# Operands of the output projection split early and stored ready-made, and the sums of w_down spread over two stages of a fused attention and GLU kernel

## The chip, the core and the metric

One core of one Trainium2 chip runs the whole kernel. The metric is the device time of one launch in microseconds (us). All arithmetic is fp32; matmuls take operands split into two fp32r parts, a high part and a rest, and form three products of these parts.

## The reference

```python
def _A_ref(x, wqkv, w_phi, wo):
    qkv = transpose((x @ wqkv).reshape(B, S, 3, H, Dh))
    q, k, v = qkv[0], qkv[1], qkv[2]
    pq = einsum("bhsd,hdf->bhsf", q, w_phi)
    pk = einsum("bhsd,hdf->bhsf", k, w_phi)
    phi_q = concat([softmax(pq), softmax(-pq)])
    phi_k = concat([softmax(pk), softmax(-pk)])
    kv = einsum("bhsf,bhsd->bhfd", phi_k, v)
    z  = einsum("bhsf->bhf", phi_k)
    num = einsum("bhqf,bhfd->bhqd", phi_q, kv)
    den = einsum("bhqf,bhf->bhq", phi_q, z)[..., None] + 1e-6
    return (num / den) reshaped to (B, S, D) @ wo
def _B_ref(x, w_gate, w_up, w_down):
    h = sigmoid(x @ w_gate) * (x @ w_up)
    return h @ w_down
xn = layernorm(x)
return x + _A_ref(xn, ...) * silu(_B_ref(xn, ...))
```

S is 2048, D is 1024, 32 heads of 32, F is 3584.

## The kernel before

Every large product is done by a seven-product scheme on 2 x 2 blocks (named B11, T2, T3, B21, T1, T4, B22). Three of the seven weight operands are raw blocks (B11, B21, T4 for the projections and wo) and four are sums of blocks (T2, T3, T1, B22). The sums are made on POOL (GpSimd), four `tensor_tensor` instructions of 128x512 for each set, and stored in HBM. An operand that comes from HBM unsplit is split just before use: `split` (L123 and L124) is a cast on ACT to the high part and a subtraction on DVE for the rest. TensorE (PE) then runs `mm3` (L128 to L130): three matmuls of 128x512 for each pair.

The work has these stages, in order of time. The sequence is two chunks of 1024 rows.

- Projections of chunk 0 (V, K, Q; 21 steps of 48 matmuls, numbered n = 0 to 20), beside which x is normalised and transposed and the weights of K and Q are folded (`fold`).
- The gated linear unit (GLU) of chunk 0: 28 units of 7 steps of 12 matmuls. Background tasks from the queue `bg` run beside it.
- Projections of chunk 1, with eight background tasks on keys (`k_task`) beside them.
- The GLU of chunk 1. Beside it run the other key tasks, and tasks from a second queue `bg2`: four `o_sums` (the sums of wo) and fourteen `wd_sums` (the sums of w_down), one at every tenth step (`m % 10 == 0`). Each loads four blocks of 256 KB, makes four sums on POOL and stores them.
- The down projection (h times w_down), 56 double steps and 14 single ones, with the attention's denominators (`q_task`) beside it.
- The attention numerators and the output projection with wo, eight pairs of row tiles.

In the down projection's last part, `wo_prep` (L607) loads each of the 28 operands of wo, raw or summed, 256 KB, into one of the two halves of slot 53 and splits it into its place. A load into a half waits until the split before it has read that half.

SBUF is a set of numbered slots of 128 x 1024 fp32, used by name of block: fa is slots 39 to 42, fb 43 to 46, fc 47 to 54, w 28 to 35 (a ring of eight slots for split weights; a projection step uses four, a GLU step one). All DMAs are issued from SP's queue, in one order. ACT, DVE, POOL and SP each take their instructions in a fixed order that a scheduler writes at build time, so an instruction that waits holds all behind it on its engine.

The names `fc<-wf_d` and `fc<-wo` in the profile are the loads of `wo_prep`; `fb<-wo` and `fb<-w_down` are those of `o_sums` and `wd_sums`; L229 to L232 and L522 to L525 are their POOL sums; `p L124` is the subtraction of the key tasks, whose results the matmuls of L448 read. L841 and L848 to L851 are POOL's work on the GLU's own results, L885 on those of the down projection.

Of the kernel before, what the change touches and what calls it, by code (L numbers as in the profile page):

```python
# [9 lines left out]
F32 = mybir.dt.float32  # L10
F32R = mybir.dt.float32r
# [6 lines left out]
P = 128  # L18
# [7 lines left out]
NJ = NF // 2  # L26
HB = 512
EPS_LN = 1e-5
EPS_DEN = 1e-6
Q, K, V, O = 0, 1, 2, 3  # L30
# [14 lines left out]
B11, T2, T3, B21, T1, T4, B22 = range(7)  # L45
# [3 lines left out]
def hedgehog_glu_kernel(  # L49
# [11 lines left out]
    nc = tc.nc  # L61
# [4 lines left out]
    dram = ctx.enter_context(tc.tile_pool(name="dram", bufs=1, space=DRAM))  # L66
# [1 line left out]
    ident = sb.tile([P, P], F32, name="ident")  # L68
    make_identity(nc, ident)

    wf_d = dram.tile([4, 7, P, 4, HB], F32, name="wf_d")
    qkv_d = dram.tile([3, TT, 2, P, HB], F32, name="qkv_d")
    xo_d = dram.tile([7, P, 4, HB], F32, name="xo_d")
    e_d = dram.tile([TT, 2, P, 2 * HB], F32, name="e_d")
# [9 lines left out]
    slots, blocks, where = {}, {}, {}  # L84
# [22 lines left out]
    def whole(i):  # L107
        return slots[i].rearrange("p a n -> p (a n)")

    def halves(*ids):  # L110
        return [slots[i][:, a] for i in ids for a in range(2)]

    def run(i, n):

        name, k = where[i]
        return blocks[name][0][:, k:k + n]

    def pair(i):
        return slots[i][:, 0], slots[i][:, 1]

    def split(o, src):

        nc.scalar.copy(o[0], src)  # L123
        return nc.vector.tensor_sub(o[1], src, o[0].bitcast(F32))  # L124
# [94 lines left out]
    fraw = Ring(halves(43, 11))  # L219
    fblock = {K: Ring(((4, 5), (6, 7))), Q: Ring(((50, 51), (52, 53)))}  # L220

    def w_sums(which, k, a11, a12, a21, a22):
        def keep(i, b):
            nc.sync.dma_start(wf_d[which, i, :, k], b)

        if which != O:
            for i, b in ((B11, a11), (B21, a12), (T4, a22)):
                keep(i, b)
        nc.gpsimd.tensor_add(a22, a21, a22)  # L229
        nc.gpsimd.tensor_sub(a21, a11, a21)  # L230
        nc.gpsimd.tensor_sub(a11, a22, a11)
        nc.gpsimd.tensor_sub(a12, a12, a11)  # L232
        for i, b in ((T2, a11), (T3, a21), (T1, a22), (B22, a12)):
            keep(i, b)
# [22 lines left out]
            nc.sync.dma_start(wf_d[V, i], row4(v_first[i]))  # L257

    def o_sums(k, bs):
        for b, (f, h) in zip(bs, ((0, 0), (0, 1), (1, 0), (1, 1))):  # L260
            nc.sync.dma_start(b, wo[(k + 4 * h) * P:(k + 4 * h + 1) * P, f * HB:(f + 1) * HB])
        w_sums(O, k, *bs)

    def fold(which, k):

        bs = halves(*fblock[which].next())
        for b, (f, h) in zip(bs, ((0, 0), (0, 1), (1, 0), (1, 1))):
            r = fraw.next()
            nc.sync.dma_start(r, wqkT[which, f, k + 4 * h].rearrange("p g n -> p (g n)"))
            ps = tps.next()  # L270
            for g in range(4):
                gs = slice(g * P, (g + 1) * P)
                nc.tensor.matmul(ps[:, gs], r[:, gs], bd[:, 4 * f + g], start=True, stop=True)
            nc.scalar.copy(b, ps)
        w_sums(which, k, *bs)


    PROJ = (V, K, Q)
# [12 lines left out]
    flow = dict(item=0, made=0, used=0)  # L291
    proj_raw = Ring((39, 41))
    gr = Ring((41, 42, 39, 40))
    sums_r = Ring(halves(43, 44))
    wraw, proj_src, last_load = {}, {}, []
    units = [(c, j, s) for c in range(NCH) for j in range(NJ) for s in range(2)]
# [3 lines left out]
    def glu_load(u):  # L300

        c, j, s = units[u]
        a = []
        for f in (j, j + NJ):
            r = gr.next()
            k = 4 if c and f != j else 0
            nc.sync.dma_start(whole(r)[:, k * P:], w_gu[f, s, :, k:].rearrange("p k m -> p (k m)"))
            a += halves(r)
        wraw[u] = a

    def glu_sums(u):
        a11, a12, a21, a22 = wraw.pop(u)
# [50 lines left out]


    u1ps, u2ps = (halves(48, 49), halves(50, 51)), (halves(45, 46), halves(48, 49))
    yps = Ring(halves(47)), Ring(halves(43, 44, 45, 46))
    last_evac = []

    def proj_out(c, which, i, u, b):

        t = c * CTT + u
        u1p, u2p, yp = u1ps[c], u2ps[c], yps[c]

        def store(th, hb, y):
            nc.sync.dma_start(qkv_d[which, t + 4 * th, hb], y)

        def evac(y, x):
            last_evac[:] = [nc.vector.tensor_add(y, x, b).ins]

        if i == B11:  # L380
            nc.scalar.copy(u1p[u], b)
        elif i == B21:
            y = yp.next()
            nc.scalar.copy(y, b)  # L384
            store(0, 0, y)
        elif i == T2:
            evac(u1p[u], u1p[u])
        elif i == T3:
            evac(u2p[u], u1p[u])
        elif i == T4:  # L390
            y = yp.next()
            evac(y, u1p[u])
            store(0, 1, y)
        elif i == T1:
            evac(u2p[u], u2p[u])
            store(1, 1, u2p[u])
        else:
            y = yp.next() if c else u1p[u]
            evac(y, u1p[u])
            store(1, 0, y)  # L400
# [42 lines left out]
    def kv_products():  # L443

        while kv_due:
            t, ph, v = kv_due.popleft()
            for g in range(8):
                nc.tensor.matmul(kvb[g // 2][:, g % 2 * 256:g % 2 * 256 + 256], v[:, g].rearrange("p a f -> p (a f)"),  # L448
                                 ph[:, g].rearrange("p a f -> p (a f)"), start=t == 0 and g % 2 == 0,
                                 stop=t == TT - 1, skip_group_check=True)  # L450
# [66 lines left out]
    def wd_sums(j, b):  # L517
        b11, b12, b21, b22 = b
        for b, i in ((b11, B11), (b12, None), (b21, B21), (b22, B22)):
            nc.sync.dma_start(b, wd_block(i, j))  # L520
        sub = nc.gpsimd.tensor_sub
        sub(b11, b12, b11)  # L522
        sub(b12, b22, b12)
        sub(b22, b22, b11)
        sub(b21, b21, b22)  # L525
        for i, b in ((T1, b11), (T3, b12), (T2, b22), (T4, b21)):
            nc.sync.dma_start(wd_d[i, j], b)
# [38 lines left out]
    def q_task(t, hb):  # L566
# [5 lines left out]
        else:  # L572
# [22 lines left out]
    KVB = (36, 37, 38, 43)  # L595
    WO = {B11: list(range(8, 12)), T2: list(range(12, 16)), T3: list(range(4, 8)), B21: [],
          T1: [], T4: [], B22: list(range(4))}
    wor = Ring([slots[53][:, 0], slots[53][:, 1]])
    phu = Ring((44, 20))
    ofr = Ring((46, 24, 25, 26, 27, 22, 23, 39, 40, 41, 42))  # L600
    res = Ring(halves(49, 52))
# [3 lines left out]
    oraw = [slots[50], slots[51]]  # L605

    def wo_prep(i, k):  # L607
        r = wor.next()
        if i in (B11, B21, T4):
            f, h = {B11: (0, 0), B21: (0, 1), T4: (1, 1)}[i]  # L610
            nc.sync.dma_start(r, wo[(k + 4 * h) * P:(k + 4 * h + 1) * P, f * HB:(f + 1) * HB])
        else:
            nc.sync.dma_start(r, wf_d[O, i, :, k])
        split(pair(WO[i][k]), r)

    def e_load(u):
        tp_, hb = divmod(e_next[u], 2)
# [136 lines left out]
    bg, bg2 = deque(), deque()  # L754
# [3 lines left out]
    for hb in range(2):  # L758
        bg.extend([lambda hb=hb, t=t: k_task(hb, t) for t in range(TT)])
        bg.extend([lambda hb=hb, f=f: f(hb) for f in (kv_sum, kv_blocks, z_broadcast)])  # L760
    bg2.extend([lambda k=k: o_sums(k, halves(43, 44)) for k in range(4)])
    bg2.extend([lambda j=j: wd_sums(j, halves(43, 44)) for j in range(NJ)])
    EARLY = 8
    tick = [0, 0]
# [1 line left out]
    def background(anchor, tasks=None):  # L766
        if tasks is None:
            tasks = bg
            kv_products()
        if tasks:  # L770
            with tc.issue_after(anchor):
                tasks.popleft()()

    for n, (kind, c, what, i) in enumerate(ops):
        ws = ready[n]
        if kind == "proj":
            for u in range(4):
                if i in opening:
                    pbank[u] = pmm.next()
                xo = run(XO[i], 4)  # L780
                us = slice(u * P, (u + 1) * P)
                for k in range(4):
                    mm3(pbank[u], (xo[:, k, 0, us], xo[:, k, 1, us]), pair(ws[k]),
                        i in opening and k == 0, k == 3, skip_group_check=True)
                step()
            flow["used"] += 4
            while prep():
                pass
            for u in range(4):
                proj_out(c, what, i, u, pbank[u])  # L790
            if c and len(bg) > 2 * (TT + 3) - EARLY and i not in (B11, B21):
                background(last_evac[0])
            continue

        j, s = what
        u = units.index((c, j, s))
# [29 lines left out]
        else:  # L826
# [8 lines left out]
            else:  # L835
                if q == 0:
                    nc.vector.tensor_mul(g, g, bank)
                else:
                    b = u1 if q == 1 else u2
# [4 lines left out]
                else:  # L844

                    a11, a21, a12, a22 = gates
# [8 lines left out]
        m = (u % (2 * NJ)) * 7 + glu_order.index(i)  # L855
        if c == 0:
            if len(bg) > 2 * (TT + 3) and i == T2 and m > 7:
                background(v.ins)
        else:
            if m >= 1 and (m - 1) % 6 == 0:  # L860
                background(v.ins)
            if m >= 10 and m % 10 == 0:
                with tc.issue_after(last_load[0]):
                    background(v.ins, bg2)
        if c == 0 and u % (2 * NJ) == 2 * NJ - 1:
# [50 lines left out]
    for n, (i, j, cs) in enumerate(dsteps):  # L916
        w, hs = dready[n]
        for c in cs:
            for u in range(4):
                p = 4 * c + u  # L920
# [15 lines left out]
        if n and n * 32 // 78 > (n - 1) * 32 // 78 and late:  # L936
            t, hb = late.pop(0)
# [48 lines left out]
    for tp_ in range(NTP):  # L986
        nxt = attend(tp_ + 1) if tp_ + 1 < NTP else []
        n = 0
        u1, u2, y11, y21 = [res.next() for _ in range(4)]
        for i in range(7):  # L990
# [3 lines left out]
            o = [h.rearrange("p (k t) -> p k t", t=P) for h in pair(of[tp_][i])]  # L994
# [12 lines left out]
            else:  # L1007
                g, xt = gxs.pop((tp_, i))
                t, cols = rows(tp_, i)
                eng = nc.vector if tp_ == NTP - 1 and i in (T4, B22) else nc.gpsimd  # L1010
                if i == B21:
                    y = y11
                    nc.vector.tensor_mul(y, g, ps)
                else:
                    y = {T1: u2, T4: y21, B22: u1}[i]
# [34 lines left out]
```

## Time and profile before

| | |
|---|---|
| median of 3 runs | 2445.2 us (2442.9 to 2446.99) |
| the profiled execution | 2443.43 us |
| its span, first to last instruction | 2441.6 us |
| PE busy | 2392.8 us, 98% of the span |
| PE's granted clock over the span | 0.995 |

Busy time of PE is the union of its matmul records, so it is not time at PE's peak. In the tables by stretch of time, a line gives start and end in us, the length, and for each engine the busy time and, in brackets, the count of instructions; then PE's granted clock, the share of DMA time and GB/s. A line of a table of groups has busy us and the mean ns of one instruction, and behind the second bar the idle time before the group and what ended it.

### The profile page before, as it was taken

The page shows a single profiled execution, that of the slowest core. Times are in us where ns is not written, and L with a number is a line of the kernel's source. Part 1 is how long each engine was busy: PE and PEld are TensorE (multiplying, and loading weights), DVE is VectorE, ACT ScalarE, POOL GpSimd, SP SyncE. Part 2 cuts the span into 40 slices and gives each one's busy share as a digit, 9 for nine tenths or more (in the row PEclk, how much of TensorE's full clock was granted, in tenths as well). Part 3 has the DMA queues.
Part 4 walks back from the last instruction along what each step waited for, and adds up shares of the span by engine and source line. Part 5 has one row for each costly group of instructions (what it writes and reads, how often), then busy time and mean ns, then how long its engine had stood idle before and what let it go on. Part 6 is the DMA issues. An engine that isn't in the chain of part 4 may idle for free.

```text
span 2441.6 us, 31984 instructions
## 1 busy us (share of the span) xinstructions
PE 2392.8 (98%) x11076; PEld 1986.7 (81%) x11076; DVE 1716.9 (70%) x2247; ACT 1001.9 (41%) x1495; POOL 987.2 (40%) x665
## 2 busy tenths in 40 slices
PE   7999999999999999999999999999999999998998
PEld 6888888888888878888888888788888888877886
DVE  6533577777776678548858888647889998765554
ACT  6432244544444344323433444423443334454332
POOL 5520146566565400004545453543333335314554
PEclk8999999999999999999999999999999999999999
DMA  7874567777776665457888887896666766755553
GB/s 280 279 255 157 195 226 261 255 257 271 263 276 242 245 216 174 172 203 249 292 301 284 275 316 257 278 339 216 217 231 219 254 218 238 236 197 191 182 182 128
DMA packets 231507, 581.61 MB, mean 238 GB/s; under 512 B 30385, under 2 KB 30385, under 8 KB 226737
## 3 DMA queue, kind: packets, MB, share of 16 engines
q1 hardware_dynamic: 231344, 579.57, 68.7%
q8 instruction: 87, 1.43, 0.2%
q14 instruction: 76, 0.61, 0.1%
HBM read 353.76 MB, written 225.71 MB: 237 GB/s over the span
## 4 chain that ended last, share of the span: by engine, by line
PE 77%; DMA 7%; DVE 6%; issue 4%; POOL 4%; ACT 2%; SPq 0%; ACTq 0%; POOLq 0%; DVEq 0%
PE bank L128 25%; PE bank L130 25%; PE bank L129 25%; DVE x L124 1%; DMA fc<-wf_d 1%; DMA w<-ws_d 1%; PE bank L448 1%; DMA fa<-w_down 1%; PE bank L627 1%; DVE w L124 1%; DMA fb<-w_down 1%; DVE p L124 1%; DMA fb<-wo 1%; ACT x L123 1%; DMA fc<-xo_d 0%
## 5 line engine op out<-in xcount | busy, mean ns | idle before, releaser
L128 PE MATMUL bank<-x,w 128*128 128x512 f32 x2352 | 912.7, 390 | 5.1 <-DVE fb L833 3.1
L129 PE MATMUL bank<-x,w 128*128 128x512 f32 x2352 | 915.9, 389 | 0.5 <-DVE x L124 0.4
L130 PE MATMUL bank<-x,w 128*128 128x512 f32 x2352 | 906.7, 389 | 0.0
L123 ACT CAST w<-fa 128x512 fp32r<-128x512 f32 (+1 forms) x444 | 308.2, 698 | 560.3 <-PE bank L129 335.8
L124 DVE TENSOR_TENSOR w<-fa,w 128x512 fp32r<-128x512 f32 (+1 forms) x444 | 434.8, 984 | 140.7 <-ACT w L123 134.1
L128 PEld LDWEIGHTS bank<-x,w 128*128 128x128 f32 x2352 | 441.6, 188 | 98.6 <-DVE fb L833 4.4
L130 PEld LDWEIGHTS bank<-x,w 128*128 128x128 f32 x2352 | 441.6, 188 | 91.9 <-DVE w L124 0.4
L129 PEld LDWEIGHTS bank<-x,w 128*128 128x128 f32 x2352 | 441.7, 188 | 91.2 <-DVE x L124 1.2
L128 PE MATMUL bank<-w,x 128*128 128x512 f32 x708 | 279.2, 394 | 3.7 <-ACT fb L384 2.1
L130 PE MATMUL bank<-w,x 128*128 128x512 f32 x708 | 278.5, 394 | 1.8 <-DVE x L124 1.8
L129 PE MATMUL bank<-w,x 128*128 128x512 f32 x708 | 277.9, 393 | 0.0
L841 POOL TENSOR_TENSOR fc<-fc 128x512 f32<-128x512 f32 x27 | 43.6, 1615 | 298.9 <-DVE fc L840 286.8
L128 PEld LDWEIGHTS bank<-w,x 128*128 128x128 f32 x708 | 134.0, 189 | 31.8 <-ACT fb L384 2.5
L130 PEld LDWEIGHTS bank<-w,x 128*128 128x128 f32 x708 | 133.8, 189 | 30.0 <-DVE x L124 2.5
L129 PEld LDWEIGHTS bank<-w,x 128*128 128x128 f32 x708 | 134.0, 189 | 27.2 <-DVE w L124 0.2
L577 POOL TENSOR_TENSOR fc<-fc 128x1024 f32<-128x1024 f32 x32 | 81.4, 2543 | 178.3 <-ACT fc L413 123.1
L841 POOL TENSOR_TENSOR fb<-fb,fc 128x512 f32<-128x512 f32 x57 | 91.2, 1600 | 130.7 <-DVE fc L840 107.3
L317 POOL TENSOR_TENSOR fb<-fa 128x512 f32<-128x512 f32 x28 | 36.7, 1309 | 248.2 <-DMA fa<-w_gu 133.7
L124 DVE TENSOR_TENSOR w<-fb,w 128x512 fp32r<-128x512 f32 (+1 forms) x114 | 106.0, 929 | 39.2 <-ACT w L123 37.7
L123 ACT CAST w<-fb 128x512 fp32r<-128x512 f32 (+1 forms) x114 | 71.4, 627 | 133.6 <-PE bank L129 103.8
L124 DVE TENSOR_TENSOR x<-fa,x 128x512 fp32r<-128x512 f32 x112 | 111.1, 993 | 15.6 <-ACT x L123 15.3
L840 DVE TENSOR_TENSOR fc<-fc,bank 128x512 f32<-128x512 f32 x84 | 57.3, 683 | 89.8 <-PE bank L130 75.8
(250 smaller groups left out, 3312.2 us busy)
## 6 DMA issues: line engine op xcount, KB each, us to landing
ws_d<-w SPq DMA_DIRECT2D x112, 512.0 KB, 3.9
w<-ws_d SPq DMA_DIRECT2D x112, 512.0 KB, 5.4
fa<-w_gu SPq DMA_DIRECT2D x84, 512.0 KB, 4.2
fa<-h_d SPq DMA_DIRECT2D x84, 512.0 KB, 4.1
fa<-wf_d SPq DMA_DIRECT2D x32, 1024.0 KB, 5.3
h_d<-fc SPq DMA_DIRECT2D x120, 256.0 KB, 4.0
fc<-e_d SPq DMA_DIRECT2D x48, 512.0 KB, 3.9
fc<-qkv_d SPq DMA_DIRECT2D x80, 256.0 KB, 4.2
```

What stands on the lines that cost most here:

```text
L123: nc.scalar.copy(o[0], src)
L124: return nc.vector.tensor_sub(o[1], src, o[0].bitcast(F32))
L128: nc.tensor.matmul(o, a[0], b[0], start=first, stop=False, **kw)
L129: nc.tensor.matmul(o, a[0], b[1], start=False, stop=False, **kw)
L130: nc.tensor.matmul(o, a[1], b[0], start=False, stop=last, **kw)
L317: nc.gpsimd.tensor_add(s1, a21, a22)
L448: nc.tensor.matmul(kvb[g // 2][:, g % 2 * 256:g % 2 * 256 + 256], v[:, g].rearrange("p a f -> p (a f)"), ph[:, g].rearrange("p a f -> p (a ...
L577: nc.gpsimd.tensor_mul(ez, e, zb)
L627: nc.tensor.transpose(ps[:, j * P:(j + 1) * P], e[:, k * P:(k + 1) * P], ident)
L840: v = nc.vector.tensor_add(b, u2 if q == 3 else u1, bank)
L841: nc.gpsimd.tensor_mul(g, g, b)
```

## The change

- `o_sums` runs in the projections of chunk 0 (after steps n = 7, 10, 13 and 16) instead of the GLU of chunk 1, and in slots 52 and 53. It now splits all seven operands of a column block itself, one after the other through slot 54, and stores each split pair (512 KB) in a new array `wo_d`. `wo_prep` becomes one load of 512 KB straight into the operand's place; its 28 casts and 28 subtractions go.
- Nine of the fourteen `wd_sums` run in the projections of chunk 1 (after B21, T2 and T1 of V, K and Q); the other five in the GLU of chunk 1, at every fourteenth step.
- The ring for the projections' results in chunk 1 shrinks from eight to six halves. The GLU weights of chunk 1 get two rings: whole slots 39 and 40, and the four halves of 41 and 42.
- What runs from `bg2` is now queued on SP behind the last store of a projection result.

```diff
-    wf_d = dram.tile([4, 7, P, 4, HB], F32, name="wf_d")
+    wf_d = dram.tile([3, 7, P, 4, HB], F32, name="wf_d")
+    wo_d = dram.tile([7, 4, P, 2 * HB], F32, name="wo_d")
...
     def o_sums(k, bs):
         for b, (f, h) in zip(bs, ((0, 0), (0, 1), (1, 0), (1, 1))):
             nc.sync.dma_start(b, wo[(k + 4 * h) * P:(k + 4 * h + 1) * P, f * HB:(f + 1) * HB])
-        w_sums(O, k, *bs)
+        def keep(i, b):
+            o = slots[54].bitcast(F32R)
+            split((o[:, 0], o[:, 1]), b)
+            nc.sync.dma_start(wo_d[i, k], whole(54))
+        w_sums(keep, *bs)
...
+    gr1, gr1h = Ring((39, 40)), Ring(halves(41, 42))
...
+        if c:
+            r, h = gr1.next(), gr1h.next()
+            nc.sync.dma_start(whole(r), w_gu[j, s].rearrange("p k m -> p (k m)"))
+            nc.sync.dma_start(h, w_gu[j + NJ, s, :, 4:].rearrange("p k m -> p (k m)"))
+            wraw[u] = halves(r) + [None, h]
+            return
...
-    yps = Ring(halves(47)), Ring(halves(43, 44, 45, 46))
+    yps = Ring(halves(47)), Ring(halves(45, 46, 47))
...
-            nc.sync.dma_start(qkv_d[which, t + 4 * th, hb], y)
+            last_load[:] = [nc.sync.dma_start(qkv_d[which, t + 4 * th, hb], y).ins]
...
     def wo_prep(i, k):
-        r = wor.next()
-        if i in (B11, B21, T4):
-            f, h = {B11: (0, 0), B21: (0, 1), T4: (1, 1)}[i]
-            nc.sync.dma_start(r, wo[(k + 4 * h) * P:(k + 4 * h + 1) * P, f * HB:(f + 1) * HB])
-        else:
-            nc.sync.dma_start(r, wf_d[O, i, :, k])
-        split(pair(WO[i][k]), r)
+        nc.sync.dma_start(slots[WO[i][k]].bitcast(F32), wo_d[i, k])
...
-    bg2.extend([lambda k=k: o_sums(k, halves(43, 44)) for k in range(4)])
+    bg2.extend([lambda k=k: o_sums(k, halves(52, 53)) for k in range(4)])
     bg2.extend([lambda j=j: wd_sums(j, halves(43, 44)) for j in range(NJ)])
...
+            if (i in (B21, T2, T1)) if c else (n % 3 == 1 and n > 5 and len(bg2) > NJ):
+                with tc.issue_after(last_load[0]):
+                    background(last_evac[0], bg2)
...
-            if m >= 10 and m % 10 == 0:
+            if m >= 14 and m % 14 == 0:
                 with tc.issue_after(last_load[0]):
                     background(v.ins, bg2)
```

More of the change, by code (lines that the diff above doesn't have):

```diff
@@ L220, in hedgehog_glu_kernel, with w_sums @@
     fblock = {K: Ring(((4, 5), (6, 7))), Q: Ring(((50, 51), (52, 53)))}
[L222 to L228, printed above, removed]
+    def w_sums(keep, a11, a12, a21, a22):
+        for i, b in ((B11, a11), (B21, a12), (T4, a22)):
+            keep(i, b)
         nc.gpsimd.tensor_add(a22, a21, a22)
@@ L274, in fold @@
             nc.scalar.copy(b, ps)
-        w_sums(which, k, *bs)
+        w_sums(lambda i, b: nc.sync.dma_start(wf_d[which, i, :, k], b), *bs)
     PROJ = (V, K, Q)
@@ L302, in glu_load @@
         c, j, s = units[u]
-        a = []
+        if c:
[4 more added lines that the diff above has]
+            return
+        wraw[u] = []
         for f in (j, j + NJ):
             r = gr.next()
[L306 to L309, printed above, removed]
+            nc.sync.dma_start(whole(r), w_gu[f, s].rearrange("p k m -> p (k m)"))
+            wraw[u] += halves(r)
     def glu_sums(u):
@@ L597, in hedgehog_glu_kernel @@
           T1: [], T4: [], B22: list(range(4))}
-    wor = Ring([slots[53][:, 0], slots[53][:, 1]])
     phu = Ring((44, 20))
```

## The prediction

> **What bounds the kernel now.** I read the table by stretch of time first, cut at the stages, then PE's waits, then the chain of waits near the end.
>
> ```profile
> core 0: us, PE busy (x) PEld busy (x) DVE busy (x) ACT busy (x) POOL busy (x), PEclk, DMA share, GB/s
> 150.00:280.00 130.00, 130.00 (x575) 107.62 (x575) 50.41 (x57) 33.36 (x39) 0.00 (x0) 1.00 0.47 160
> 280.00:860.00 580.00, 580.00 (x2592) 480.89 (x2591) 417.45 (x556) 260.99 (x385) 334.57 (x226) 1.00 0.72 255
> ...
> 880.00:950.00 70.00, 70.00 (x325) 58.58 (x324) 65.80 (x82) 30.86 (x37) 0.00 (x0) 1.00 0.56 189
> 950.00:1097.00 147.00, 147.00 (x665) 122.33 (x664) 85.64 (x107) 45.57 (x53) 0.00 (x0) 1.00 0.52 179
> 1097.00:1330.00 233.00, 229.87 (x1053) 190.29 (x1053) 174.91 (x213) 94.22 (x130) 108.64 (x72) 1.00 0.81 280
> 1330.00:1600.00 270.00, 265.48 (x1217) 219.83 (x1217) 213.76 (x251) 114.82 (x154) 129.84 (x87) 1.00 0.84 287
> ...
> 2135.00:2196.00 61.00, 58.09 (x287) 46.97 (x286) 42.57 (x61) 35.13 (x64) 11.67 (x8) 1.00 0.59 198
> 2196.00:2257.00 61.00, 54.06 (x291) 44.18 (x290) 33.48 (x48) 24.69 (x45) 25.57 (x19) 1.00 0.59 190
> ...
> sum 2441.60, PE 2392.80 PEld 1986.66 DVE 1716.88 ACT 1001.87 POOL 987.23; mean PE 184.06 PEld 152.82 DVE 132.07 ACT 77.07 POOL 75.94
> ```
>
> TensorE is the bound: 2392.8 of 2441.6 us. The change adds and removes no matmul, so it can only win part of the 48.8 us in which PE stands idle, or add to them. The stages that it touches hold these parts: nothing in the later projections of chunk 0 (150 to 280) and in the projections of chunk 1 (880 to 1097), where PE is full; 3.1 and 4.5 us in the GLU of chunk 1 (233 - 229.87 and 270 - 265.48); 2.9 and 6.9 us around the end of the down projection (61 - 58.09 and 61 - 54.06). Together 17.4 us, which is the ceiling of any gain. The change takes work out of the two stages with idle PE and puts it into two stages where PE is full, and POOL there is at 0.00.
>
> **End of the down projection: what the 28 splits cost.** PE's waits from 2196 to 2257, ACT's waits in the same stretch, and a piece of the chain:
>
> ```profile
> PE bank L128 <- ACT fa L123: 1.7, 1, 1.7
> PE bank L128 <- DVE x L911: 1.6, 1, 1.6
> PE bank L128 <- DVE fc L1016: 1.1, 1, 1.1
> PE bank L128 <- ACT w L123: 1.0, 1, 1.0
> PE bank L128 <- ACT fb L123: 0.8, 1, 0.8
> PE bank L130 <- DVE fa L124: 0.6, 1, 0.6
> ...
> ACT x L123 <- DMA fc<-wf_d: 15.8, 4, 5.6
> ACT w L123 <- DMA fc<-wf_d: 4.1, 1, 4.1
> ```
> ```profile
> 2210.36 0.32 SPq L889
> ...
> 2210.78 4.62 DMA fc<-wf_d
> ...
> 2215.49 0.63 ACT x L123
> ...
> 2216.14 0.70 DVE x L124
> ...
> 2216.86 3.12 DMA fc<-wf_d
> ```
>
> ACT stands for 15.8 + 4.1 = 19.9 of 61 us at casts of `wo_prep` whose load has not landed. All behind them on ACT waits too: the casts of attention operands (fa, fb) for which PE waits. SP is held the same way: a load into a half of slot 53 goes only after the subtraction that reads it, and one turn of that loop took 2216.86 - 2210.78 = 6.08 us, 4.62 of it the landing and 1.46 the rest. The new `wo_prep` has no cast, no subtraction and no half to wait for. So of the six waits only the 1.6 on L911 (the last evacuation of the down projection) stays: 1.7 + 1.1 + 1.0 + 0.8 + 0.6 = 5.2 us go. Of the 2.9 idle us before 2196, where the same loop runs among the loads of w_down and h, I take half, 1.4. What is late next: the four direct loads of B22 go into slots 0 to 3 and wait for the last stores of the down projection, of which SP issues the last at 2210.36 (row above). A load of 512 KB takes about 5.4 us (row below).
>
> ```profile
> ws_d<-w SPq DMA_DIRECT2D x112, 512.0 KB, 3.9
> w<-ws_d SPq DMA_DIRECT2D x112, 512.0 KB, 5.4
> fb<-wo SPq DMA_DIRECT2D x16, 256.0 KB, 6.8
> ...
> 2200.52 0.50 PE L128 MATMUL bank<-x,fb 128*128 128x512 f32 x1 [1.60 <-DVE x L911]
> ```
>
> With 3.9 for the store's landing they leave at some 2210.4 + 3.9 = 2214.3 and land by 2220 to 2222. The output projection begins at 2200.5 and eight pairs fill the rest of the span, 241 / 8 = 30 us each; B22 is the last of seven products, so it is due near 2200.5 + 30 * 6/7 = 2226. That is 4 us to spare, so I take off a little: the stage gives **-6 us**, between -8 (all 2.9 go as well) and -1 (these loads, or those of T3 ahead of the h loads on SP, hold PE instead).
>
> **GLU of chunk 1.** PE's waits from 1097 to 1600, one of them looked at on POOL and DVE, and the same DVE instruction without POOL (950 to 1100) and beside it (1160 to 1560):
>
> ```profile
> PE bank L448 <- DVE p L124: 3.2, 4, 1.3
> PE bank L128 <- DVE fb L833: 3.1, 3, 2.4
> ...
> 1503.22 2.15 POOL L525 TENSOR_TENSOR fb<-fb 128x512 f32<-128x512 f32 x1
> ...
> 1504.15 2.31 DVE L124 TENSOR_TENSOR p<-fc,p 128x1024 fp32r<-128x1024 f32 x1
> ```
> ```profile
> L124 DVE TENSOR_TENSOR p<-fc,p 128x1024 fp32r<-128x1024 f32 x4 | 4.9, 1216 | 0.0
> L378 DVE TENSOR_TENSOR fc<-fc,bank 128x512 f32<-128x512 f32 x22 | 15.0, 684 | 15.8 <-PE bank L130 15.6
> ...
> L124 DVE TENSOR_TENSOR p<-fc,p 128x1024 fp32r<-128x1024 f32 x20 | 33.1, 1653 | 0.0
> L840 DVE TENSOR_TENSOR fc<-fc,bank 128x512 f32<-128x512 f32 x28 | 19.1, 683 | 26.2 <-PE bank L130 21.6 <-POOL fb L841 3.2 <-POOL fc L841 1.2
> ```
>
> PE waits for DVE, and DVE is late because POOL slows it: 1216 ns become 1653 on average and 2310 where a sum of w_down runs at that moment. An instruction with a PSUM operand keeps its 684 ns. The change takes four `o_sums` and nine `wd_sums` out of here, 52 POOL instructions, and their 104 DMAs. After step 70 no task of `bg2` is left, so of the 4.5 us after 1330 I take 2.7; before it five tasks run in place of seven, and I take 0.8 of 3.1. POOL's work on gates stays, and can delay DVE as before. **-3.5 us**, between -7 and 0. The new rings for the GLU weights only let the half loads go earlier; I cost them at nothing, hidden by the w ring.
>
> **Projections of chunk 0.** They get 16 loads, 16 sums, 28 casts, 28 subtractions and 28 stores. The engines have room: ACT is at 33 of 130 us, DVE at 50, POOL at 0, DMA at 0.47. The question is order. All 28 go through slot 54 in series, and a cast that waits for the store before it holds ACT, and with it the casts of the projection weights. One turn is the landing plus the 1.46 above: with 3.9 for a 512 KB store, 5.4 us. In the changed order on ACT, 22 pieces of projection weights (11 steps) stand between the first and the 21st of these casts. The cast of such a piece, before:
>
> ```profile
> L123 ACT CAST w<-fa 128x1024 fp32r<-128x1024 f32 x22 | 23.1, 1054 | 69.5 <-PE bank L130 69.4
> ```
>
> A step is 48 matmuls of 130 / 575 = 0.226 us, 10.85 us, so 11 steps take 119 us and 20 turns 107 us: the chain keeps up. Moreover a piece is ready some 2.4 us after its slot comes free (1054 ns of cast and near 1.2 us of subtraction; ACT waits for nothing but PE here) and due a step later, so some 8.4 us of delay cost nothing. The seven other turns stand between GLU pieces, of which eight are ready ahead. **+1 us**, between 0 and the rival below.
>
> **Projections of chunk 1.** Nine `wd_sums`: 36 loads, 36 sums on an idle POOL, 36 stores with DMA at 0.52 to 0.56. The sums slow DVE, which from 880 to 950 is busy for 65.8 of 70 us. Three tasks, 12 sums, fall there. At worst each costs one DVE instruction 2.31 - 1.22 = 1.09 us, together 13; I take half, 6.5. Against it stand DVE's 4.2 idle us and its lead:
>
> ```profile
> 947.20 1.22 DVE L124 TENSOR_TENSOR w<-fa,w 128x1024 fp32r<-128x1024 f32 x1
> ...
> 954.14 1.05 ACT L123 CAST w<-fa 128x1024 fp32r<-128x1024 f32 x1 [0.30 <-PE bank L130]
> ```
>
> The subtraction for the step that begins when PE returns slots at 954.1 ended at 948.4: 5.7 us of lead. So 6.5 us are covered by 9.9, and 13 are not, by 3. **+0.5 us**, between 0 and +3. After 950 DVE has 61 idle us of 147. SP queues the stores behind POOL's sums; the loads of projection weights behind them have a whole step of 10.85 us.
>
> **Sum.** -6 - 3.5 + 1 + 0.5 = -8. The profiled execution took 2443.4 us, so 2435.4; the median of the runs shown is 1.8 above that execution, and I forecast a median of 2437.2. About 0.2%, 5 us, is what a measurement of this kernel can tell from no change.
>
> **Rivals.** (1) *Slower: the chain through slot 54 sets the pace of chunk 0.* The landing decides: 20 turns fit into 119 + 8.4 us up to 4.9 us of landing. The 3.9 speaks against it, and it was taken mostly in the GLU of chunk 0, with the DMA share at 0.72; for it speak the 5.4 and 6.8 us of other transfers. At 5.4 the turns take 137 us, +10; at 6.8 they take 165 us, +38. With the gains of -9 elsewhere: 2446 to 2474, some 2456 in the middle. Chance 0.13.
>
> (2) *The waits only change hands.* The direct loads are twice as large and late by what the splits were, and DVE stays late by POOL's gate work: only some 3 us go, 2442. For it speaks that PE's waits in the GLU are short and many and that each has another instruction behind it. Chance 0.20.
>
> (3) *DVE in chunk 1 is held for whole sums.* If each of the 12 sums between 880 and 950 held DVE for its full 2.15 us (row above), that is 26 us, 16 past the cover of 9.9: 2445.2 - 9 + 16 = 2452. Against it speaks the mean of 1653, less than half of such a delay on one instruction. Chance 0.07. The Trainium skill, "SBUF — State Buffer", Who interferes with whom, states such a rule: a DVE instruction with two SBUF inputs and a GpSimd instruction that reads SBUF exclude each other for the whole instruction, whereas one with a single SBUF input does not contend. By that rule this case decides; the trace agrees on who is affected (1216 to 1653 ns with two SBUF operands, 684 and 683 with a PSUM operand), and on the size only at single instructions (2310).
>
> **Numbers.** The forecast has 0.60 and by itself 2430 to 2442: its ends are the full gains (-8 - 7) and gains of half size. Range 2430 to 2448, which takes in rival 2 and the lower part of rival 1. Faster 0.62 (the forecast and a little of rival 2), within 0.2% 0.22, slower 0.16 (most of rivals 1 and 3).
>
> **What would show it.** Right: no ACT wait for a load of wo after 2100 and PE idle near 3.5 us in the two stretches around the end of the down projection; in the GLU of chunk 1 the p subtraction nearer to 1216 ns and PE idle near 4 us; PE still full in both projection stages. Wrong: PE idle between 150 and 300 with ACT casts in fc that wait for a store to wo_d (rival 1); PE waits for the subtraction of w between 880 and 960 (rival 3); new PE waits on B22's load in the first pair (rival 2).

## The result, and the profile after

The changed kernel takes 2438.51 us (median of 20 runs, 2429.96 to 2443.7), the kernel before 2446.1 us (20 runs, 2442.9 to 2449.2): a ratio of 0.997, with a 95% interval of 0.9962 to 0.9978. That is 7.6 us less, and 1.3 us above the forecast. The profiled execution has a span of 2436.6 us at a granted clock of 0.996 (before 2441.6 us, 0.995).

The total came out as predicted, the parts did not: the loss in chunk 0 and the gains in the other stages were all far larger than forecast, and they offset each other. Here is the table by stretch of time of the changed kernel, in the stretches that were shown of before (line numbers are up to ten higher than before: the splits are L124 and L125, the three matmuls L129 to L131). Its stages begin up to 13 us later than before, so a stretch does not hold quite the same work.

```profile
core 0: us, PE busy (x) PEld busy (x) DVE busy (x) ACT busy (x) POOL busy (x), PEclk, DMA share, GB/s
150.00:280.00 130.00, 126.32 (x552) 103.04 (x551) 59.44 (x70) 40.91 (x56) 19.49 (x13) 1.00 0.72 242
280.00:860.00 580.00, 574.36 (x2560) 474.64 (x2560) 416.93 (x568) 259.69 (x385) 332.97 (x227) 1.00 0.75 264
...
880.00:950.00 70.00, 67.81 (x307) 55.31 (x306) 64.95 (x75) 28.09 (x32) 19.81 (x12) 1.00 0.81 278
950.00:1097.00 147.00, 146.97 (x668) 122.17 (x667) 100.17 (x111) 43.93 (x54) 38.48 (x24) 1.00 0.78 261
1097.00:1330.00 233.00, 231.55 (x1060) 192.21 (x1059) 176.08 (x217) 102.84 (x138) 85.95 (x58) 1.00 0.79 266
1330.00:1600.00 270.00, 270.00 (x1246) 225.08 (x1245) 206.45 (x257) 117.96 (x157) 77.55 (x52) 1.00 0.66 218
...
2135.00:2196.00 61.00, 59.21 (x296) 48.98 (x295) 36.43 (x53) 31.22 (x56) 9.05 (x7) 1.00 0.64 219
2196.00:2257.00 61.00, 61.00 (x336) 52.37 (x335) 30.80 (x42) 21.56 (x38) 28.53 (x21) 1.00 0.74 255
```

Idle PE (length less busy time) goes down from 3.1 and 4.5 to 1.5 and 0 us in the GLU of chunk 1, and from 2.9 and 6.9 to 1.8 and 0 around the end of the down projection. It goes up from 0 to 3.7 and 5.6 in chunk 0, and from 0 to 2.2 between 880 and 950.

Idle time understates a stall, though, and a second view shows it. These are the waits of PE's weight loads from 2196 to 2280 in the kernel before (first fence) and in the changed one (second): what is waited for, us in total, times, longest.

```profile
PEld bank L128 <- ACT fa L123: 2.5, 2, 2.2
PEld bank L128 <- DVE x L911: 1.8, 1, 1.8
PEld bank L128 <- ACT w L123: 1.4, 1, 1.4
PEld bank L128 <- DVE fc L1016: 1.3, 1, 1.3
PEld bank L128 <- ACT fb L123: 1.2, 1, 1.2
PEld bank L130 <- DVE fa L124: 1.1, 2, 0.9
...
```
```profile
PEld bank L630 <- DVE x L125: 0.9, 1, 0.9
PEld bank L131 <- DVE x L125: 0.7, 1, 0.7
```

The first is cut after its six largest rows, 9.3 us, against 1.6 us after. The same six rows are 6.8 us in the matmul rows that the prediction used. Why they differ is seen at any wait of PE, such as this one in the changed kernel:

```profile
290.05 0.39 PE L131 MATMUL bank<-w,x 128*128 128x512 f32 x1
291.07 0.50 PE L129 MATMUL bank<-w,x 128*128 128x512 f32 x1 [0.63 <-DVE fc L388]
```

The starts are 1.02 us apart where 0.226 us is the pace, so 0.79 us are lost; but the first record lasts until 290.44, and 0.63 us are shown as idle. Each wait loses some 0.16 us from view in this way, and waits shorter than that don't show at all.

So I measure the stages by landmarks instead: the first and the last copy of a B11 bank in the projections of chunk 1, and the first such copy in the down projection. The first pair is of the kernel before, the second of the changed one; the columns behind the count are the durations in ns (minimum, median, maximum) and the first and last start.

```profile
L381 ACT COPY fc<-bank x12: 568/578/589, 844.6 to 1012.5; 128x512 f32<-128x512 f32 x12
...
L896 ACT COPY x<-bank x8: 579/587/589, 1720.5 to 1726.0; 128x512 f32<-128x512 f32 x8
```
```profile
L391 ACT COPY fc<-bank x12: 568/582/589, 857.5 to 1026.3; 128x512 f32<-128x512 f32 x12
...
L902 ACT COPY x<-bank x8: 579/588/589, 1726.4 to 1731.8; 128x512 f32<-128x512 f32 x8
```

The four stages, in us, for this and, read in the same way, for all kernels of the experiments below:

| kernel | A: start to first B11 copy of chunk 1 | B: to the last (Q) | C: GLU of chunk 1, to the first B11 copy of the down projection | D: from there to the end | span |
|---|---|---|---|---|---|
| before | 844.6 | 167.9 | 708.0 | 721.1 | 2441.6 |
| changed | 857.5 (+12.9) | 168.8 (+0.9) | 700.1 (-7.9) | 710.2 (-10.9) | 2436.6 (-5.0) |
| two slots | 846.2 | 172.6 | 699.8 | 708.1 | 2426.7 |
| wo alone | 853.2 | 167.6 | 704.7 | 709.8 | 2435.3 |
| w_down alone | 845.4 | 170.0 | 703.0 | 723.8 | 2442.2 |
| before, no sums beside GLU | 845.2 | 167.4 | 697.9 | 721.3 | 2431.8 |
| two slots, no sums of w_down | 846.5 | 169.9 | 698.0 | 708.8 | 2423.2 |
| two slots, sums in K and Q | 845.4 | 165.7 | 702.6 | 708.5 | 2422.2 |
| changed, no sums of wo | 853.5 | 171.0 | 700.2 | 707.3 | 2432.0 |
| two slots again | 845.3 | 170.6 | 700.2 | 708.5 | 2424.6 |

Each is one execution. How far a stage differs between executions can be read where the code is the same: A is 844.6 to 846.5 without the single slot, and 853.2 to 857.5 with it; D is 721.1 to 723.8 with the splits at the end, and 707.3 to 710.2 without.

Two of the 12.9 us in A were lost before the first of the new casts ran (it starts at 159.08). This is the first B11 copy of K in chunk 0, before and in the changed kernel:

```profile
147.31 0.59 ACT L381 COPY fc<-bank 128x512 f32<-128x512 f32 x1 [1.66 <-PE bank L130]
```
```profile
149.31 0.59 ACT L391 COPY fc<-bank 128x512 f32<-128x512 f32 x1 [1.67 <-PE bank L131]
```

With two slots it starts at 149.05, so this part is not the slot's. From this copy to the end of A it is 696.5 to 697.3 us in the seven executions without the single slot, and 708.2 (changed), 705.7 (wo alone) and 705.3 (changed, no sums of wo) with it. The chain through the slot thus cost 10.9 us here, and 8.0 to 8.4 in the other two.

Where these 10.9 us went is seen in ScalarE's waits from 150 to 340 and in a piece of its timeline. The timeline's columns are start, duration, engine, line, instruction, and in brackets the idle time before it and what ended it.

```profile
ACT fc L124 <- DMA wo_d<-fc: 91.1, 23, 8.2
ACT fc L124 <- POOL fc L229: 9.4, 2, 4.8
ACT fc L394 <- DMA qkv_d<-fc: 6.3, 1, 6.3
...
311.80 0.62 ACT L124 CAST fc<-fc 128x512 fp32r<-128x512 f32 x1 [7.30 <-DMA wo_d<-fc]
...
315.19 0.62 ACT L124 CAST w<-fb 128x512 fp32r<-128x512 f32 x1 [1.21 <-POOL fb L328]
315.72 0.58 ACT L827 COPY fc<-bank 128x512 f32<-128x512 f32 x1
...
324.47 0.62 ACT L124 CAST fc<-fc 128x512 fp32r<-128x512 f32 x1 [5.96 <-DMA wo_d<-fc]
...
326.93 0.60 ACT L837 ACTIVATE fb<-bank 128x512 f32<-128x512 f32 x1
```
```profile
316.35 0.50 PE L129 MATMUL bank<-x,w 128*128 128x512 f32 x1 [1.81 <-ACT fc L827]
```

And PE's waits from 150 to 380 (before, there was none):

```profile
PE bank L129 <- DVE fc L388: 2.7, 4, 1.4
PE bank L129 <- ACT fb L837: 2.3, 1, 2.3
PE bank L129 <- ACT fc L394: 1.8, 2, 1.2
PE bank L129 <- ACT fc L827: 1.8, 1, 1.8
PE bank L129 <- DVE fb L388: 0.6, 1, 0.6
```

That is 9.2 us in nine waits; with the 0.16 us that each hides it is 10.6, near the 10.9.

Of 28 casts into slot 54, 23 wait for the store of the one before, 91.1 us together. Each such wait holds all that stands behind it on ScalarE: the cast at 311.80 stood for 7.30 us, the bank copy of L827 came behind it at 315.72, and at 316.35 PE, which had waited 1.81 us for that bank, went on. The activation of L837 behind the next held cast cost PE 2.3 us in the same way. All five rows are evacuations that free a bank; none is a weight piece. Those of L388 run on VectorE, which is held in its turn: its subtractions wait for the same casts for 65.5 us, in 21 waits. The casts are not the whole of it everywhere: between the cast at 311.80 and the copy at 315.72 stand 1.21 us of wait for POOL, and a copy of L394, for which PE waited 1.23 us, had itself waited 6.3 us for the store of a projection result (third row of the first fence).

### The profile page after: what moved, and what is told of

The parts are those of the page before. It is cut to its first block, busy times and chain, and to the rows that moved or that the text cites. A ratio compares the mean times of both kernels' runs of the same rounds, so it can differ in the third digit from the quotient of the medians.

```text
span 2436.6 us, 32010 instructions
## 1 busy us (share of the span) xinstructions
PE 2389.2 (98%) x11076; PEld 1984.5 (81%) x11076; DVE 1717.3 (70%) x2247; ACT 1006.8 (41%) x1499; POOL 989.3 (41%) x665
## 4 chain that ended last, share of the span: by engine, by line
PE 74%; DMA 7%; DVE 7%; issue 5%; POOL 4%; ACT 2%; SPq 0%; ACTq 0%; POOLq 0%; DVEq 0%
PE bank L129 24%; PE bank L131 24%; PE bank L130 24%; DMA wo_d<-fc 3%; DVE w L125 1%; PE bank L458 1%; DVE x L125 1%; PE bank L630 1%; DVE p L125 1%; DMA fb<-wqkT 1%; DMA fc<-xo_d 1%; PE bank L278 0%; DVE fc L125 0%; DMA out<-fc 0%; DMA fc<-wo 0%
## 5 line engine op out<-in xcount | busy, mean ns | idle before, releaser
L129 PE MATMUL bank<-x,w 128*128 128x512 f32 x2352 | 912.8, 390 | 8.0 <-ACT fb L837 2.3
L131 PE MATMUL bank<-x,w 128*128 128x512 f32 x2352 | 907.1, 389 | 0.0
L129 PEld LDWEIGHTS bank<-x,w 128*128 128x128 f32 x2352 | 441.5, 188 | 102.9 <-ACT fb L837 2.7
L131 PEld LDWEIGHTS bank<-x,w 128*128 128x128 f32 x2352 | 441.6, 188 | 92.0 <-DVE w L125 0.4
L124 ACT CAST w<-fa 128x512 fp32r<-128x512 f32 (+1 forms) x444 | 307.6, 697 | 504.7 <-PE bank L130 371.0
L125 DVE TENSOR_TENSOR w<-fa,w 128x512 fp32r<-128x512 f32 (+1 forms) x444 | 438.5, 992 | 108.7 <-ACT w L124 101.6
L129 PE MATMUL bank<-w,x 128*128 128x512 f32 x708 | 279.5, 395 | 7.8 <-DVE fc L388 3.2
L131 PE MATMUL bank<-w,x 128*128 128x512 f32 x708 | 277.8, 393 | 1.8 <-DVE x L125 1.8
L129 PEld LDWEIGHTS bank<-w,x 128*128 128x128 f32 x708 | 133.8, 189 | 38.9 <-DVE fc L388 3.4
L131 PEld LDWEIGHTS bank<-w,x 128*128 128x128 f32 x708 | 133.5, 189 | 29.8 <-DVE x L125 2.5
L125 DVE TENSOR_TENSOR x<-fa,x 128x512 fp32r<-128x512 f32 x112 | 114.7, 1024 | 18.0 <-ACT x L124 17.9
L125 DVE TENSOR_TENSOR w<-fb,w 128x512 fp32r<-128x512 f32 (+1 forms) x114 | 102.4, 899 | 32.8 <-ACT w L124 31.1
L124 ACT CAST w<-fb 128x512 fp32r<-128x512 f32 (+1 forms) x114 | 71.3, 626 | 118.7 <-PE bank L130 97.0
L599 POOL TENSOR_TENSOR fc<-fc,sa 128x1024 f32<-128x1024 f32 x32 | 70.4, 2199 | 101.1 <-DVE sa L596 101.1
```

The lines of the kernel that those rows point to most:

```text
L129: nc.tensor.matmul(o, a[0], b[0], start=first, stop=False, **kw)
L131: nc.tensor.matmul(o, a[1], b[0], start=False, stop=last, **kw)
L599: nc.gpsimd.tensor_mul(e3, e3, r2[:, :, None].to_broadcast([P, 32, DH]))
```

## Experiments

My theory after these views: the change gains in C and D and loses in A, and the loss is the single staging slot, not the added work. The rivals were that the added DMA traffic or POOL's sums in chunk 0 are to blame, and, for C, that the DMAs and not the sums had slowed the GLU. The first four kernels ran on one chip, with the kernel before at 2443.51 us (23 runs); the other four on one chip with it at 2446.87 us (11 runs).

**Two slots for the split pairs.** The pairs alternate between slots 54 and 51; nothing else differs from the changed kernel.

```diff
+    keep_r = Ring((54, 51))
...
-            o = slots[54].bitcast(F32R)
+            s = keep_r.next()
+            o = slots[s].bitcast(F32R)
             split((o[:, 0], o[:, 1]), b)
-            nc.sync.dma_start(wo_d[i, k], whole(54))
+            nc.sync.dma_start(wo_d[i, k], whole(s))
```

> The changed kernel with the split pairs of wo going alternately through slots 54 and 51, nothing else altered. If the series through one slot is what holds ACT (23 waits, 91.1 us, of a cast for the store before it), these waits fall below 30 us, PE's idle time between 150 and 380 us falls from 9.3 us to 2 or less, and the time is 6 to 8 us below the changed kernel, near 2431. If it is instead the added work and traffic itself (28 splits, 19 MB more in this stage), PE idle there stays near 9 us and the time near 2438.

Measured: 2424.4 us (2423.68 to 2428.56, 6 runs), a ratio to before of 0.9927 (0.9912 to 0.9942). Stage A fell to 846.2 us. The table by stretch:

```profile
150.00:280.00 130.00, 130.00 (x575) 107.67 (x574) 69.15 (x84) 49.28 (x67) 25.63 (x17) 1.00 0.84 293
280.00:380.00 100.00, 100.00 (x447) 82.90 (x446) 68.88 (x92) 39.10 (x60) 50.30 (x35) 1.00 0.71 252
```

PE is full from 150 to 380, with the same 28 casts, sums and stores; the DMA share is 0.84 up to 280 (0.72 in the changed kernel), and 0.78 over the whole of 150 to 380 (0.77). So neither the traffic nor the sums by themselves cost anything there; the single slot does. ScalarE's waits for these stores were 35.9 us in 14 waits, more than expected, and PE is full all the same. The gain is larger than I had expected of it, and the interval lies clear of the changed kernel's 0.9962 to 0.9978.

**wo alone.** The changed treatment of wo, with the sums of w_down and the rings as before.

```diff
-            if (i in (B21, T2, T1)) if c else (n % 3 == 1 and n > 5 and len(bg2) > NJ):
+            if not c and (n % 3 == 1 and n > 5 and len(bg2) > NJ):
...
-            if m >= 14 and m % 14 == 0:
+            if m >= 10 and m % 10 == 0:
```

> Only the wo part of the change: operands split beside the projections of chunk 0, direct loads; all fourteen sums of w_down stay in the GLU of chunk 1 at every tenth step, and the rings of chunk 1 are those of before. If the parts add up: -8 at the end of the down projection, +9 in chunk 0, and in the GLU some -2, since four of eighteen tasks go; about 2445, no change. If the loss in chunk 0 were smaller than read from the one profile, near 2439.

Measured: 2438.61 us (2433.89 to 2444.5, 12 runs), ratio 0.998 (0.9969 to 0.9991). A is 853.2, D 709.8 and C 704.7 us: the loss of A, the gain of D, and 3.3 us in C for the four sets of wo that left the GLU. It was expected at 1 us less than before and came out 4.9 less. The loss in A was as large as I had read it (+8.6 for 9); what I had too small were the gains, D at -8 (measured -11.3) and C at -2 (-3.3).

**w_down alone.** The sums of w_down as changed, wo as before: `o_sums` without splits in the GLU, and the old `wo_prep` with its 28 splits.

```diff
-            if (i in (B21, T2, T1)) if c else (n % 3 == 1 and n > 5 and len(bg2) > NJ):
+            if c and i in (B21, T2, T1):
...
-        nc.sync.dma_start(slots[WO[i][k]].bitcast(F32), wo_d[i, k])
+        r = wor.next()
...
+        split(pair(WO[i][k]), r)
```

> Only the w_down part: nine sums of w_down beside the projections of chunk 1, then the four of wo and the other five of w_down in the GLU at every fourteenth step; wo is loaded and split at the end as before. If the parts add up: +2 in the projections of chunk 1, -4 to -6 in the GLU, nothing at the end (9.8 idle us there as before); about 2442. If the gain of the GLU needs the removal of wo's sums, no change, 2446.

Measured: 2441.63 us (2435.98 to 2447.19, 12 runs), ratio 0.9992 (0.9981 to 1.0003). That is 1.9 us less than before on this chip, where 4 less was expected; the interval takes in both that and no change. C is 703.0 (-5.0 for nine sets that left the GLU), B 170.0 (+2.1). The two halves of the change add up within their intervals: 0.998 and 0.9992 make 0.9972, the whole has 0.997.

**Before, without POOL's sums beside the GLU of chunk 1.** The four POOL sums of each set of wo and of w_down are left out; all their loads and stores stay, and unsummed blocks are stored.

```diff
-        nc.gpsimd.tensor_add(a22, a21, a22)
+        if which != O:
+            nc.gpsimd.tensor_add(a22, a21, a22)
...
-        sub(b11, b12, b11)
```

> The kernel before, with the POOL sums of wo and w_down in the GLU of chunk 1 left out and all their loads and stores kept (their operands are then raw blocks). If PE's 7.6 idle us there come from POOL holding DVE: they fall to 2 or less, the key tasks' subtraction of 128x1024 falls from 1653 ns towards 1300, and the DMA share stays near 0.8. If they come from the 144 DMAs: PE idle stays at 6 us or more though POOL is free.

Measured once: 2433.54 us, span 2431.8.

```profile
1097.00:1330.00 233.00, 233.00 (x1073) 194.32 (x1072) 172.27 (x216) 99.16 (x134) 66.00 (x45) 1.00 0.83 288
1330.00:1600.00 270.00, 270.00 (x1243) 224.90 (x1242) 199.76 (x252) 116.64 (x156) 69.00 (x47) 1.00 0.85 295
...
L124 DVE TENSOR_TENSOR p<-fc,p 128x1024 fp32r<-128x1024 f32 x20 | 32.0, 1602 | 0.0
```

PE is full with a DMA share of 0.83 and 0.85 (before 0.81 and 0.84): the sums cost the GLU its 10.1 us in C (708.0 to 697.9), the DMAs nothing. But the mean of the p subtraction, which I had taken as the sign of it, hardly moved (1653 to 1602 ns; 1216 where POOL did nothing). What is left on POOL here, 66.0 and 69.0 us of work on the gates for the most part, is enough to slow it on average. What went are single coincidences that PE waited for: in the kernel before, three of PE's four waits for p come behind a p subtraction of 2.30 to 2.32 us that ran beside a sum of wo or w_down (the one at 1150.52 beside L231 and L232). For the 3.1 us of waits at L833 the trace shows no such pair: the longest, 2.4 us, has gate work alone beside VectorE just before it. They too are gone without the sums; by which way is not shown.

**Two slots, without the sums of w_down.** Loads and stores stay, unsummed blocks are stored (here and in the GLU).

```diff
-        sub(b11, b12, b11)
-        sub(b12, b22, b12)
-        sub(b22, b22, b11)
-        sub(b21, b21, b22)
```

> Two slots for the split pairs (as in the first experiment), and of every set of w_down the four POOL sums left out: the loads and stores stay in their places, and the blocks are stored unsummed. With the sums in place TensorE was idle for 2.7 us between 880 and 950, 1.3 between 1097 and 1330. Theory (the sums slow VectorE, which makes the weights late): idle between 880 and 950 falls to 0.7 us or less, the p subtraction of 128x1024 stays at its 1.22 us, time about 2421. Rival (the 12 loads and 12 stores of three sets, in SP's order ahead of other loads): idle there stays between 2 and 3 us, time about 2424.

Measured once: 2425.02 us, span 2423.2. PE's idle time between 880 and 950 is 2.0 us, against 2.7 and 3.6 in the two executions with the sums, and B is 169.9 against 172.6 and 170.6 (before 167.9). So the idle time came out at the edge of what the rival expected (2 to 3): in this one execution most of the loss in B stays without the sums. The split of the weights, and the loads of folded weights from 880 to 950, in this kernel and then in the one with the sums (two slots again):

```profile
L125 DVE TENSOR_TENSOR w<-fa,w 128x1024 fp32r<-128x1024 f32 x11 | 13.4, 1215 | 0.0
...
fa<-wf_d SPq DMA_DIRECT2D x6, 1024.0 KB, 7.5
```
```profile
L125 DVE TENSOR_TENSOR w<-fa,w 128x1024 fp32r<-128x1024 f32 x12 | 16.8, 1400 | 0.0
...
fa<-wf_d SPq DMA_DIRECT2D x6, 1024.0 KB, 5.9
```

The sums do slow DVE, by 185 ns an instruction (some 2.2 us over 12 of them), and at most a part of that reaches PE, whose idle time falls by 0.7 to 1.6 us without them. The rest of the loss could come through the added transfers, by loads that land later. VectorE's waits for the casts of x, which themselves wait for the load `fc<-xo_d`, from 870 to 950 in the kernel before, in this one without sums, and in the one with them (two slots again):

```profile
DVE x L124 <- ACT x L123: 2.9, 1, 2.9
```
```profile
DVE x L125 <- ACT x L124: 9.2, 3, 5.9
```
```profile
DVE x L125 <- ACT x L124: 3.1, 1, 3.1
```

The first two fit that reading, the third does not: with sums and transfers together this wait is as short as before, and PE's idle time is the largest of all, 3.6 us (the first execution of the same kernel had 9.6 us of this wait and 2.7 of idle time). So what makes up the rest of the loss in B stays open; single executions differ by as much as 1 to 2 us here.

**Two slots, sums in K and Q.** No set of w_down beside V; six beside K and Q, eight in the GLU instead of five.

```diff
-            if (i in (B21, T2, T1)) if c else (n % 3 == 1 and n > 5 and len(bg2) > NJ):
+            if (what != V and i in (B21, T2, T1)) if c else (n % 3 == 1 and n > 5 and len(bg2) > NJ):
```

> Two slots, all work done, and no set of w_down in the steps of V in chunk 1: six sets in those of K and Q, eight in the GLU instead of five. Theory (the sums cost TensorE time only where VectorE is full, 65 of 70 us between 880 and 950, and not where it has 47 of 147 us idle): idle between 880 and 950 falls from 2.7 to below 1 us, 950 to 1097 stays at 0, the GLU from 1097 to 1600 rises from 1.3 to 2 to 3 us by three more sets; net -1, about 2423.4. Rival (the eight key tasks beside V are what makes VectorE late there, with or without sums): idle stays above 2, the GLU rises by 1 to 2, time 2425 to 2426.

Measured: 2426.95 us (2424.0 to 2428.47, 5 runs), ratio 0.9921 (0.9908 to 0.9933).

```profile
880.00:950.00 70.00, 69.08 (x319) 57.24 (x318) 65.00 (x81) 31.37 (x37) 0.22 (x1) 1.00 0.60 202
950.00:1097.00 147.00, 147.00 (x665) 122.28 (x664) 94.31 (x108) 46.38 (x54) 36.86 (x24) 1.00 0.76 262
```

The stages went as the theory has it: idle time between 880 and 950 is 0.9 us with VectorE just as busy (65.0 of 70), and B 165.7; the GLU's idle time is 3.4 us, a little more than expected, and C 702.6. Beside the two-slot kernel run again, that is -4.9 us in B and +2.4 in C, so half of the gain in B is given back in the GLU. The medians do not show the other half: the time is not 1 us below that of the other two-slot kernel, but the same (2426.17 beside it). The profiled executions were the fastest of five here and the slowest of five there. VectorE's load by itself was not the loss in B: it is the same with and without the three sets.

**The changed kernel without the sums of wo.** One slot; the four POOL sums of each set of wo are left out, all loads, splits and stores stay.

```diff
-        nc.gpsimd.tensor_add(a22, a21, a22)
+        if sums:
+            nc.gpsimd.tensor_add(a22, a21, a22)
...
-        w_sums(keep, *bs)
+        w_sums(keep, *bs, sums=False)
```

> The changed kernel (one slot for the split pairs) with the four POOL sums of every set of wo left out: loads, casts, subtractions and stores of all 28 operands stay, the blocks are stored unsummed. Tells what in a turn of 6.3 to 6.4 us is the landing of the store and what is the wait for POOL (9.4 us in two waits on ScalarE between 150 and 340). If the landing alone sets the pace: the 27 turns still take 165 to 172 us and TensorE is idle for 8 to 10 us between 150 and 380. If the wait for POOL is what the forecast missed: the turns take about 160 us and the idle falls to 5 us or less.

Measured once: 2433.78 us, span 2432.0. The first and the last of the 28 casts:

```profile
159.12 0.62 ACT L124 CAST fc<-fc 128x512 fp32r<-128x512 f32 x1 [1.21 <-DMA fc<-wo]
...
322.87 0.62 ACT L124 CAST fc<-fc 128x512 fp32r<-128x512 f32 x1 [0.37 <-DMA wo_d<-fc]
```

27 turns in 163.8 us, 6.06 each, and 5.6 us of idle PE between 150 and 380: between the two expectations. Stage A is 853.5, still 8.9 us longer than before (8.0 from the first copy of K on), so the stores alone cost most of it. Whether the wait for POOL is the rest stays open, because the two executions with the sums lie at 853.2 and 857.5.

**Two slots again**, beside the kernel with the sums in K and Q.

> The two-slot kernel once more, beside the kernel with the sums in K and Q on the same chip, since the two should differ by 1 us only. Theory: 2424.4 again within 1 us, with TensorE idle for 2 to 3 us between 880 and 950 and for none between 150 and 380.

Measured: 2426.17 us (2424.84 to 2426.39, 5 runs), ratio 0.9917 (0.9904 to 0.993). PE is full from 150 to 380 again; idle between 880 and 950 is 3.6 us, more than the 2 to 3 expected. The time is 1.8 us above the first, where 1 was expected at most, while before was 3.4 us higher there.

## Why the prediction was right, and where it was not

The time and the sign were right; the sum of -8 was right by luck, because a loss and two gains that were each mis-sized offset each other. By its own steps:

- **Projections of chunk 0: +1 forecast, +12.9 in the profiled execution, 10.9 of it by the chain (8.4 with wo alone).** This is the step that failed; what happened is the mechanism of rival 1, which had a chance of 0.13. Four things were wrong in it. First, the turn. I put it at 5.4 us, from the median landing of 3.9 us and 1.46 us around it. The median landing of the new stores is indeed 3.7 us, but the 28 range from 2.6 to 8.3, and their mean is 4.4:

```profile
L265 SPq DMA_DIRECT2D wo_d<-fc x28: 319/320/965, 160.5 to 330.6; - x28
...
DMA to landing us min/median/max: 2.6/3.7/8.3
...
159.08 0.62 ACT L124 CAST fc<-fc 128x512 fp32r<-128x512 f32 x1
...
329.20 0.62 ACT L124 CAST fc<-fc 128x512 fp32r<-128x512 f32 x1 [0.64 <-DMA wo_d<-fc]
```

  The 27 turns took 170.1 us, 6.30 each: 4.4 of landing, 1.6 from the start of a cast to the issue of its store, 0.3 from the landing to the next cast. A chain in series goes by the mean of its links, not by their median. Second, the cover. I compared the chain with the weight pieces that stand between its casts. What PE waited for were the evacuations that stand there too, copies and activations that free a bank (L388, L394, L827, L837), and a late bank has no lead of 8.4 us. For the first 20 turns the limit of 127.4 us (119 + 8.4) was nevertheless near the mark: they took 128.5 us in the changed kernel, with 3.7 us of idle PE up to 280, 124.9 with wo alone (1.0 idle) and 122.7 without the sums of wo (0.7 idle). Third, and most, I said that the seven last turns cost nothing because eight GLU pieces are ready ahead. Between 280 and 340 PE stood idle for 5.6 of 9.3 us, for 5.4 of 6.4 with wo alone and for 4.9 of 5.6 without the sums of wo, again for late evacuations. Fourth, the splits' fourth cast of a set, which waits for three POOL sums, was not in the sum at all: 9.4 us of ScalarE's time in two waits, some 5.4 of them past the landing of the store before.
- **End of the down projection: -6 forecast, -10.9 (to -13.8 in the two-slot and other kernels with the direct loads, by stage D).** The mechanism was right: no cast waits for a load of wo, and the loads of B22, issued from 2216.8 on and landed in 3.3 to 7.2 us, hold nobody. All six waits are gone, also the 1.6 us on L911 that I had expected to stay. The size was off, beyond its bound of -8, because I summed PE's idle rows. The rows of the weight loads show 10.4 us of stall from 2196 to 2280 before (all ten rows) and 1.6 after, 8.8 of the 10.9. From 2135 to 2196 they fall from 5.9 to 3.2 us, and from 1720 to 2135 they rise from 1.8 to 3.8; the rest stays open.
- **GLU of chunk 1: -3.5 forecast, -7.9 by stage C, just past its bound of -7.** Right in kind: without any sums C is 10.1 us shorter, and the DMAs cost nothing. Per set the runs give 0.55 (nine sets fewer, -5.0) to 0.8 us (four sets fewer, -3.3), so that the thirteen sets that left are worth 7 to 11 us; I had counted idle PE there too, and discounted it by half. The sign that I named for it was wrong: the p subtraction went from 1653 to 1581 ns only, not towards 1216.
- **Projections of chunk 1: +0.5 forecast, +0.9 in the profiled execution,** and +2.1 to +4.7 in the other executions with three sets beside V, so the upper bound of +3 is about the usual price. PE did not stay full, as I had it. The reason given (12 sums slow DVE) is a part of it at most: with the sums left out, B was still 2.0 us longer than before, in one execution, and what makes up that part is open.
- **Rival 2** (waits only change hands) is refuted by D and C. **Rival 3** (VectorE held for whole sums, at worst 16 us) did not happen: the w subtraction is at 1513 ns in the changed kernel and 1400 with two slots, beside the sums, and 1215 without. The Trainium skill, "SBUF — State Buffer", Who interferes with whom, says that DMA uses ports of its own and never contends with a compute engine. The trace agrees: the 1215 ns stand beside a DMA share of 0.78; before, the w subtraction took 1210 at 0.56, and the p subtraction of the same size 1216 at 0.52.
- **The range** reached 2448 to take in the lower part of rival 1. With the measured gains beside it (-18.8 in C and D in place of -9), that rival came out at the forecast and not above it.

## What to carry to other kernels

Where several transfers go one after another through one staging buffer, cost the chain by the mean landing, list everything that stands behind the waiting instruction on its engine, evacuations of accumulator banks above all, and ask first whether a second buffer is free: here it was worth 11.3 us in stage A, more than the whole change. Size a stall by the distance between two landmarks, or by the waits of the weight loads: PE's idle time left some 0.16 us of every wait out here. Of a slowdown by contention, look for the single instructions that the bottleneck waits for; the mean of a group need not move when they go.

## What was not expected of the hardware

- The landing of one and the same store (512 KB, SBUF to HBM, SP's queue) goes from 2.6 to 8.3 us within 170 us, with a median of 3.7 and a mean of 4.4.
- The times of one kernel spread by 13.7 us over 20 runs of the changed kernel and 10.6 over 12 of wo alone. The single slot is not shown to be the reason: w_down alone, without it, has 11.2 over 12 runs, and the kernel before has 6.3, 12.2 and 9.4 (20, 23 and 11 runs).
